# Grouping attention's PV matmuls by four column tiles, with new rules for ordering work and for sharing it with VectorE

## The chip, the cores and the metric

The kernel runs on one core of one Trainium2 chip. The metric is device time in microseconds (us), measured per execution; each figure is a median over several executions. On one core, a run is called slow when it is over 1.5% above the fastest run of the same kernel in its rounds. A profile is the record of one execution, and its span is a few us shorter than the measured time (965.3 against 967.4 us before). The profiled execution of the kernel before took 967.4 us, more than the median given below. "Granted clock" is TensorE's clock as the profile records it, as a share of full speed: the records hold only 1.00 and 0.50.

## The reference

One multi-query attention (32 query heads of width 16, one shared key and value head) over 2048 tokens of width 512, multiplied by a gate from a SwiGLU feed-forward network on the same normalised input:

```python
def _A_ref(x, wq, wk, wv, wo):            # S=2048, D=512, H=32, Dh=16
    q = (x @ wq).reshape(B, S, H, Dh).transpose(0, 2, 1, 3)
    k, v = x @ wk, x @ wv
    scores = jnp.einsum("bhqd,bkd->bhqk", q, k) * (Dh ** -0.5)
    p = softmax(scores, axis=-1)
    o = jnp.einsum("bhqk,bkd->bhqd", p, v)
    return o.transpose(0, 2, 1, 3).reshape(B, S, H * Dh) @ wo

def _B_ref(x, w_gate, w_up, w_down):      # F=1792
    return (silu(x @ w_gate) * (x @ w_up)) @ w_down

xn = layernorm(x)
return x + _A_ref(xn, ...) * silu(_B_ref(xn, ...))
```

All inputs are bfloat16.

## The kernel before

The attention runs in 32 blocks (16 groups of eight heads by 512 queries, each in two halves of four heads) of 16 steps, one step per 128 keys. A step makes two score tiles of 128x1024: four small matmuls, each with a contraction of 32 rows, so that they sit in four row groups of TensorE's array. The score tiles go into three ring buffers in PSUM. Most tiles are turned into probabilities by ScalarE (an exponential, written as bfloat16 into one of eight buffers `Pb`). Some go to VectorE, which builds the exponential from bit operations and two products: two score reads (`passA`), two masks (`dM`, `dE`) and two products (`dQ`, `dC`) for a pair of tiles, and three terms that the PV matmuls add up. The PV matmuls are 128x32: each uses 32 columns of the array, and four of them, one for each head, can sit in four column tiles (in the trace four that start together take 0.33 us, of the score matmuls as of PV, see below).

The order of instructions on each engine is fixed when the kernel is built, by a small list scheduler in the kernel's own Python. It knows a duration for each operation, and picks by priority (lower first): score matmuls and VectorE's score reads 0, exponentials, PV and the evictions of the feed-forward's PSUM bank 1, the "fill" matmuls of the feed-forward and projections 2.

```python
class _Sched:
    LAT = 0.13          # between two operations that depend on each other
    SWITCH = 0.09       # TensorE changes its kind of matmul
    ...
    def _pick(self, e):
        ...
        tm = max(t, min(o.ready for o in lst))
        best = min((o for o in lst if o.ready <= tm + 1e-9), key=lambda o: (o.prio, o.seq))
        if e in ("PE", "DVE"):
            soon = [o for o in lst if o.ready <= tm + 0.12 and o.prio[0] < best.prio[0]]
            if soon:
                best = min(soon, key=lambda o: (o.prio, o.seq))
        return max(t, best.ready), best
```

The loop over score tiles (k is the tile, two for each step) decides which tile VectorE gets, and issues PV as soon as one exponential is done, two matmuls at a time:

```python
        bl = sd.backlog["DVE"] + max(0.0, sd.free["DVE"] - now)
        if k >= 40 and st["last_d"] < k - 1:
            if st["d_half"] is None:
                if t <= BLK_T_D and bl < 2.5:
                    isD = True
            elif x != st["d_half"][0]:
                if bl < 2.5 or t >= NT - 3:
                    isD = True
        ...
        if not isD:
            ...
            ex = OP("ACT", 0.905, [scop, pdep, prev_exp], ..., name="exp")
            mms = [(VA[:, t, DH * half:DH * half + GRP], Pb[i][:, u * 512:(u + 1) * 512], 2 * x + u) for u in range(2)]
            pv = OP("PE", 0.23, [ex, o_rel[0], vdep], pv_emit(b, mms), (1, k), f"c{x}", "pv")
        else:
            ...   # passA; with the second tile of a pair also dM, dE, dQ, dC and twelve PV matmuls
```

The fill matmuls all go through one PSUM bank, `m_ps`: after four or more of them an eviction by ScalarE (tanh) and VectorE has to run before the next can start.

## Time and profile before

Before the change the median was 960.36 us over three runs (956.92 to 967.58).

| | before |
|---|---|
| span of the trace | 965.3 us |
| busy: TensorE, ScalarE, VectorE | 88%, 88%, 66% |
| score tiles on ScalarE, on VectorE | 868, 156 |
| mean granted clock | 0.949 |
| changes of kind on TensorE (score, PV, fill), from the instruction order; the trace gives the same | 2028 |

The first lines are the page's busy times and shares, and its 40 slices of the span. A digit is a tenth of a slice; `PEclk` is the granted clock in tenths.

```profile
PE 852.6 (88%) x5568; PEld 247.6 (26%) x5665; DVE 636.7 (66%) x771; ACT 850.3 (88%) x946; POOL 52.9 (5%) x64
...
ACT  2678798999999999999989999999999999799770
...
PEclk9858899999999999999999999999999999798795
```

Busy shares say that two engines are equally loaded, and not what their work costs. For this one reads starts. The timeline of the kernel before, around 405 us (columns: start, length, engine, line, operation, output and inputs, shape, count):

```profile
402.65 1.06 ACT L777 ACTIVATE Pb_126<-ring_97 128x1024 bf16<-128x1024 f32 x1
...
403.55 1.07 ACT L777 ACTIVATE Pb_127<-ring_98 128x1024 bf16<-128x1024 f32 x1
...
404.99 0.39 PE L763 MATMUL ring_98<-QB_119,KT_85 32*128 32x512 bf16 x2
...
405.31 0.39 PE L666 MATMUL o_ps<-Pb_127,VA 128*32 128x512 bf16 x2
...
405.63 0.39 PE L763 MATMUL ring_97<-QB_119,KT_85 32*128 32x512 bf16 x2
405.64 0.39 PE L763 MATMUL ring_96<-QB_119,KT_85 32*128 32x512 bf16 x2
...
405.96 0.39 PE L666 MATMUL o_ps<-Pb_128,VA 128*32 128x512 bf16 x2
```

An exponential is shown as 1.06 us long, but the next starts 0.90 us after it: the cost of one is 0.903 us, the smallest distance of two starts in the trace. On TensorE two score matmuls (404.99) hold the engine for 0.32 us until two PV matmuls start (405.31), which hold it for 0.32 us too. At 405.63 four score matmuls go together, in four row groups, and cost 0.33 us: as much as two. What runs side by side is nearly free here (0.33 us for four, 0.32 for two). Call a run of matmuls of one kind a **visit**, and its cost the smallest distance from its start to the start of the next kind; longer distances hold a wait, or matmuls that follow one another instead of starting together (in some visits of four PV matmuls of this trace the second two start 0.23 us after the first two, and the visit takes 0.54 us). A visit of two PV matmuls costs 0.325 us, one of four in four column tiles 0.331 us, one of twelve 0.764 us. Twelve are three sets of four, so a set takes about 0.21 us, which leaves about 0.11 us for each change of kind (both are estimates from 0.331 and 0.764 us).

With 0.903 us for an exponential and 0.477 for a tanh, ScalarE's work is 868 x 0.903 + 72 x 0.477 = 818 us. The first exponential starts at 20.5 us and the last at 934.7, so 914.2 us hold about 817 us of work. The other 97 us are **gaps**: the sum, over all pairs of ScalarE instructions between the first and the last exponential, of the distance of their starts less 0.903 us (or 0.477 us after a tanh).

The chain that ended last, by engine and by line, is the third view. PV matmuls (`o_ps L666`) are its largest item:

```profile
PE 52%; DVE 23%; ACT 9%; issue 7%; DMA 4%; SPq 3%; POOL 0%; DVEq 0%; ACTq 0%; POOLq 0%
PE o_ps L666 19%; PE m_ps L555 7%; PE ring_97 L763 6%; PE ring_98 L763 6%; PE ring_96 L763 6%; DVE Ub_129 L796 4%; PE m_ps L575 4%; DVE Ub_130 L796 3%; SPq L714 3%; DVE Wb_134 L814 2%; PE m_ps L442 1%; ACT th_135 L560 1%; DVE Wb_134 L817 1%; DVE Wb_133 L814 1%; ACT Pb_121 L777 1%
```

Last, stretches of time: busy us and number of instructions of each engine, then the granted clock.

```profile
core 0: us, PE busy (x) PEld busy (x) DVE busy (x) ACT busy (x) POOL busy (x), PEclk, DMA share, GB/s
0.00:118.00 118.00, 91.10 (x554) 27.72 (x562) 64.11 (x122) 78.29 (x88) 14.06 (x36) 0.83 0.23 78
...
300.00:500.00 200.00, 184.48 (x1227) 53.77 (x1246) 132.53 (x151) 192.32 (x216) 11.14 (x8) 1.00 0.05 12
500.00:700.00 200.00, 186.73 (x1271) 54.74 (x1290) 145.64 (x164) 192.75 (x216) 9.71 (x7) 1.00 0.04 10
```

In the middle TensorE is busy 92 to 93% and its clock is full. (Some matmul records are missing from this trace: 5568 matmuls against 5665 weight loads, so counts of matmuls in it are a little low.)

### The profile page before, as it was taken

How to read it: one execution, taken by the hardware profiler on the slowest of the kernel's cores; microseconds unless marked ns; L12 is line 12 of the kernel's file. 1: busy time of each engine (PE TensorE's matmuls, PEld its weight loads, DVE VectorE, ACT ScalarE, POOL GpSimd, SP SyncE). 2: the span in 40 equal slices, each digit the busy share in tenths (PEclk: the TensorE clock that was granted, in tenths of full speed). 3: DMA queues.
4: the chain of work that ended last, by engine and by line, in shares of the span. 5: the costliest groups of instructions: out<-in, count | busy, mean ns of one | idle time of the engine just before them, and what ended most of it. 6: DMA issues, size and time to landing. Idle time of an engine off the chain costs nothing.

```text
span 965.3 us, 14557 instructions
## 1 busy us (share of the span) xinstructions
PE 852.6 (88%) x5568; PEld 247.6 (26%) x5665; DVE 636.7 (66%) x771; ACT 850.3 (88%) x946; POOL 52.9 (5%) x64
## 2 busy tenths in 40 slices
PE   3799898988999999999989899998989999898980
PEld 1322222222222222222222222222222222222220
DVE  6416887878763567666775688897553558787553
ACT  2678798999999999999989999999999999799770
POOL 3100000000000100000000010000000110000001
PEclk9858899999999999999999999999999999798795
DMA  9000000000000100000000100000000000000001
GB/s 333 28 1 1 18 2 18 1 7 12 2 19 6 29 6 18 3 1 18 1 18 7 30 6 7 13 2 18 1 18 6 18 18 2 18 1 18 1 1 42
DMA packets 20109, 18.62 MB, mean 19 GB/s; under 512 B 9024, under 2 KB 15936, under 8 KB 20032
## 3 DMA queue, kind: packets, MB, share of 16 engines
q1 hardware_dynamic: 18448, 17.05, 5.8%
q8 instruction: 46, 0.75, 0.3%
q10 hardware_dynamic: 1584, 0.56, 0.2%
q14 instruction: 31, 0.25, 0.1%
HBM read 12.88 MB, written 2.36 MB: 16 GB/s over the span
## 4 chain that ended last, share of the span: by engine, by line
PE 52%; DVE 23%; ACT 9%; issue 7%; DMA 4%; SPq 3%; POOL 0%; DVEq 0%; ACTq 0%; POOLq 0%
PE o_ps L666 19%; PE m_ps L555 7%; PE ring_97 L763 6%; PE ring_98 L763 6%; PE ring_96 L763 6%; DVE Ub_129 L796 4%; PE m_ps L575 4%; DVE Ub_130 L796 3%; SPq L714 3%; DVE Wb_134 L814 2%; PE m_ps L442 1%; ACT th_135 L560 1%; DVE Wb_134 L817 1%; DVE Wb_133 L814 1%; ACT Pb_121 L777 1%
## 5 line engine op out<-in xcount | busy, mean ns | idle before, releaser
L666 PEld LDWEIGHTS <-VA 128*32 128x32 bf16 x1736 | 76.6, 94 | 185.7 <-issue 185.0
L763 PEld LDWEIGHTS <-KT_84 32*128 32x128 bf16 x1024 | 46.0, 92 | 168.4 <-issue 162.7
L763 PEld LDWEIGHTS <-KT_85 32*128 32x128 bf16 x1024 | 44.9, 91 | 158.0 <-issue 156.6
L555 PE MATMUL m_ps<-xnT,wg_sb 128*128 128x512 bf16 x204 | 65.7, 397 | 6.7 <-issue 2.4
L555 PE MATMUL m_ps<-xnT,wu_sb 128*128 128x512 bf16 x186 | 60.2, 389 | 9.3 <-DVE ab_137 L562 3.2
L575 PE MATMUL m_ps<-wd_sb,hT 128*128 128x512 bf16 x193 | 62.0, 392 | 4.9 <-issue 4.8
L796 DVE TENSOR_SCALAR Ub_130<-ring_98 128x1024 uint16<-128x1024 f32 x35 | 42.8, 1222 | 27.2 <-PE ring_98 L763 21.1
L796 DVE TENSOR_SCALAR Ub_129<-ring_97 128x1024 uint16<-128x1024 f32 x29 | 35.4, 1222 | 25.1 <-PE ring_97 L763 23.1
L814 DVE TENSOR_TENSOR Wb_134<-Wb_134 128x2048 f16<-128x2048 f16 x39 | 51.5, 1321 | 0.0
L817 DVE TENSOR_TENSOR Wb_134<-Wb_134,Ub_130 128x2048 f16<-128x2048 f16 x39 | 50.1, 1285 | 1.1
L796 DVE TENSOR_SCALAR Ub_129<-ring_98 128x1024 uint16<-128x1024 f32 x30 | 36.6, 1221 | 21.0 <-PE ring_98 L763 18.8
L777 ACT ACTIVATE Pb_121<-ring_98 128x1024 bf16<-128x1024 f32 x38 | 40.1, 1056 | 10.5 <-PE ring_96 L763 5.8
L777 ACT ACTIVATE Pb_125<-ring_97 128x1024 bf16<-128x1024 f32 x40 | 42.4, 1060 | 6.8 <-PE ring_97 L763 6.5
L814 DVE TENSOR_TENSOR Wb_133<-Wb_133 128x2048 f16<-128x2048 f16 x39 | 48.4, 1241 | 0.0
L817 DVE TENSOR_TENSOR Wb_133<-Wb_133,Ub_129 128x2048 f16<-128x2048 f16 x39 | 47.3, 1213 | 0.8
L777 ACT ACTIVATE Pb_121<-ring_96 128x1024 bf16<-128x1024 f32 x37 | 39.0, 1054 | 9.7 <-PE ring_97 L763 9.3
L777 ACT ACTIVATE Pb_122<-ring_96 128x1024 bf16<-128x1024 f32 x43 | 45.3, 1053 | 1.8 <-PE ring_98 L763 1.0
L666 PE MATMUL o_ps<-Pb_123,VA 128*32 128x512 bf16 x218 | 44.8, 408 | 0.6 <-DVE oa_138 L711 0.2
L777 ACT ACTIVATE Pb_127<-ring_96 128x1024 bf16<-128x1024 f32 x41 | 43.9, 1071 | 1.6 <-PE ring_96 L763 1.1
L666 PE MATMUL o_ps<-Pb_121,VA 128*32 128x512 bf16 x218 | 44.9, 408 | 0.3 <-DVE oa_138 L711 0.2
L666 PE MATMUL o_ps<-Pb_125,VA 128*32 128x512 bf16 x216 | 44.4, 408 | 0.7 <-DVE oa_139 L711 0.5
L666 PE MATMUL o_ps<-Pb_122,VA 128*32 128x512 bf16 x218 | 45.0, 410 | 0.0
(161 smaller groups left out, 2004.6 us busy)
## 6 DMA issues: line engine op xcount, KB each, us to landing
rb_142<-dscr_147 SPq DMA_DIRECT2D x8, 256.0 KB
rb_142<-dscr_148 SPq DMA_DIRECT2D x8, 256.0 KB
wg_sb<-in_B_w_gate_dram SPq DMA_DIRECT2D x1, 1792.0 KB
wu_sb<-in_B_w_up_dram SPq DMA_DIRECT2D x1, 1792.0 KB
wd_sb<-in_B_w_down_dram SPq DMA_DIRECT2D x1, 1792.0 KB, 19.8
x_sb<-in_A_x_dram SPq DMA_DIRECT2D x3, 512.0 KB
oa_138<-oa_139 SPq DMA_DIRECT2D x32, 32.0 KB, 2.0
oa_140<-oa_141 SPq DMA_DIRECT2D x32, 32.0 KB, 2.0
```

Source lines behind the costliest of these rows:

```text
L442: return [nc.tensor.matmul(out=dst, lhsT=wq_sb[:, kc, jj * P:(jj + 1) * P], rhs=xnT[:, kc, qs * 512:(qs + 1) * 512], start=(kc == 0), stop ...
L555: return lambda: [nc.tensor.matmul(out=m_ps[:], lhsT=w[:, kc, f * P:(f + 1) * P], rhs=xnT[:, kc, sc * 512:(sc + 1) * 512], start=(kc == 0) ...
L560: t_ = OP("ACT", 0.48, [a], lambda: nc.scalar.activation(out=th[i][:], in_=m_ps[:], func=ACT.Tanh, scale=0.5), (0,), name="tanh")
L575: return lambda: [nc.tensor.matmul(out=m_ps[:, :D], lhsT=hT[:, f, tt * P:(tt + 1) * P], rhs=wd_sb[:, f, :], start=(f == 0), stop=(f == FC ...
L666: r.append(nc.tensor.matmul(out=o_ps[GRP * g:GRP * g + GRP, :], lhsT=lhs, rhs=rhs, start=(n == 0), stop=(n == pv_total[(b, g)] - 1), tile_ ...
L714: return [nc.sync.dma_start(out=dn[DH * (2 * g + half):DH * (2 * g + half) + DH, pair, :], in_=oat[GRP * g + r0:GRP * g + r0 + 1, :]) for ...
L763: r.append(nc.tensor.matmul(out=tile_ps[:, u * 512:(u + 1) * 512], lhsT=KT[half][GRP * g:GRP * g + GRP, t * P:(t + 1) * P], rhs=QB[pair % ...
L777: ex = OP("ACT", 0.905, [scop, pdep, prev_exp], lambda i=i, tile_ps=tile_ps: nc.scalar.activation(out=Pb[i][:], in_=tile_ps[:], func=ACT.E ...
L796: pa = OP("DVE", 1.16, [scop, udep], lambda ui=ui, x=x, tile_ps=tile_ps: nc.vector.tensor_scalar(out=Ub[ui][:, x * 1024:(x + 1) * 1024], i ...
L814: e3 = OP("DVE", 1.16, [e1], lambda ei=ei: nc.vector.tensor_tensor(out=Wb[ei][:].bitcast(FP16), in0=Wb[ei][:].bitcast(FP16), in1=Wb[ei][:] ...
L817: e4 = OP("DVE", 1.16, [e3], lambda ui=ui, ei=ei: nc.vector.tensor_tensor(out=Wb[ei][:].bitcast(FP16), in0=Wb[ei][:].bitcast(FP16), in1=Ub ...
```

## The change

The intent has three parts. (1) **Joining**: PV matmuls are issued only in fours. In a step that ScalarE does alone, its two tiles are joined. In a step that it shares with VectorE it has only one tile, and that one is kept until the next shared step brings the other half. (2) **Picking rules**: TensorE and VectorE look ahead for a coming score operation (priority 0) and start other work only if this delays it by at most 2.0 us or 0.2 us; a dependence inside VectorE or GpSimd counts 0.08 us (before 0.13 us). On TensorE the limit of 2.0 us never binds, because the longest single operation in its plan counts about 1 us: in effect TensorE no longer idles up to 0.12 us for a coming score matmul. (3) **Share**: VectorE gets a tile whenever its queue of planned work is below 4.0 us (before 2.5, and not two tiles in a row).

```diff
 class _Sched:
+    SAME = {"DVE": 0.08, "POOL": 0.08}
+    GUARD = {"PE": 2.0, "DVE": 0.2}
...
-            lat = 0.0 if d.eng == op.eng == "PE" else self.LAT
+            lat = self.LAT if d.eng != op.eng else self.SAME.get(op.eng, 0.0)
...
-        if e in ("PE", "DVE"):
-            soon = [o for o in lst if o.ready <= tm + 0.12 and o.prio[0] < best.prio[0]]
-            if soon:
-                best = min(soon, key=lambda o: (o.prio, o.seq))
+        if e in self.GUARD:
+            hot = [o for o in lst if o.prio[0] <= 0 and o.ready > tm]
+            if hot and best.prio[0] > 0:
+                h = min(hot, key=lambda o: (o.ready, o.seq))
+                lim = h.ready + self.GUARD[e]
+                fit = [o for o in lst if o.ready <= tm + 1e-9 and tm + o.dur + self._sw(o) <= lim]
+                best = min(fit, key=lambda o: (o.prio, o.seq)) if fit else h
...
+    D_START, D_BL = 20, 4.0
...
-        if k >= 40 and st["last_d"] < k - 1:
-            if st["d_half"] is None:
-                if t <= BLK_T_D and bl < 2.5:
-                    isD = True
-            elif x != st["d_half"][0]:
-                if bl < 2.5 or t >= NT - 3:
-                    isD = True
+        if s >= D_START:
+            if st["d_half"] is None:
+                if t <= NT - 4 and bl < D_BL:
+                    dx = 0
+            elif bl < D_BL or t >= NT - 2:
+                dx = 1 - st["d_half"][0]
...
-            pv = OP("PE", 0.23, [ex, o_rel[0], vdep], pv_emit(b, mms), (1, k), f"c{x}", "pv")
+        todo = None
+        if dx is None:
+            todo = exps
+        elif half_pv is None:
+            half_pv = exps
+        else:
+            todo = dict(half_pv)
+            todo.update(exps)
+            half_pv = None
+        if todo is not None:
+            ...
+            pv = OP("PE", 0.25, [todo[x][0] for x in todo] + [o_rel[0], v_ready[c]], pv_emit(b, mms), (1, s), "c", "pv")
```

The rest of the diff rewrites the loop from tiles to steps and is left out.

More of the change, by code (lines that the diff above doesn't have):

```diff
@@ L209, in _arm, with _sw @@
         self.ready[op.eng].append(op)
+    def _sw(self, o):
+        return self.SWITCH if o.eng == "PE" and self.mode is not None and o.mode[0] != self.mode else 0.0
     def _pick(self, e):
@@ L646 @@
     st = {"d_half": None, "last_d": -9, "nA": 0, "nU": 0, "u": None, "nd": 0, "d0": None, "ev": None}
-    def slot_for(k):
-        best, bt = None, None
-        for i in range(3):
-            o = ring_rel[i]
-            t = o.end if o.start is not None else 1e6 + ring_age[i]
-            if best is None or t < bt:
-                best, bt = i, t
-        return best
     def pv_emit(b, mms):
@@ L670, in pv_emit @@
         return f
-    NB = NSC * NQ * 2
-    BLK_T_D = NT - 4
-    pend = {"norm": []}
+    D_START, D_BL = 20, 4.0
     ffn_list = []
@@ L728, in finish_block, with mm_of @@
             o_ready[pair // NQ] = m_
-    k = 0
     prev_exp = None
-    while k < NTILE:
-        b = k // TPB
-        t = (k % TPB) // 2
-        x = k % 2
+    half_pv = None
+    def mm_of(buf, w, i, t, half, gs):
+        r = []
+        for g in gs:
+            lhs = VA[:, t, DH * half:DH * half + GRP] if i is None else VD[:, i, t, DH * half:DH * half + GRP]
+            r.append((lhs, buf(g), g))
+        return r
+    for s in range(NTILE // 2):
+        b, t = s // NT, s % NT
         pair, half = b // 2, b % 2
-        if k % TPB == 0:
-            blk = {"pvs": [], "gcount": [0, 0, 0, 0]}
+        if t == 0:
+            pvs = []
+            half_pv = None
@@ L739 @@
             st["d_half"] = None
-        while gi < len(gates) and gates[gi][0] <= k:
+        while gi < len(gates) and gates[gi][0] <= 2 * s:
             gates[gi][2]()
             gi += 1
-        remaining = TPB - (k % TPB)
-        isD = False
         now = sd.free["PE"]
         bl = sd.backlog["DVE"] + max(0.0, sd.free["DVE"] - now)
-        if k >= 40 and st["last_d"] < k - 1:
+        dx = None
+        if s >= D_START:
             if st["d_half"] is None:
-                if t <= BLK_T_D and bl < 2.5:
-                    isD = True
-            elif x != st["d_half"][0]:
-                if bl < 2.5 or t >= NT - 3:
-                    isD = True
@@ L754 @@
-        c = t // 4
-        sl = slot_for(k)
-        tile_ps = ring[sl]
-        deps = [ring_rel[sl], k_ready[c][half], q_ready[pair]]
-        def sc_emit(tile_ps=tile_ps, x=x, t=t, half=half, pair=pair):
-            r = []
-            for u in range(2):
-                g = 2 * x + u
-                r.append(nc.tensor.matmul(out=tile_ps[:, u * 512:(u + 1) * 512],
-                                          lhsT=KT[half][GRP * g:GRP * g + GRP, t * P:(t + 1) * P],
-                                          rhs=QB[pair % 2][GRP * g:GRP * g + GRP, :],
-                                          start=True, stop=True, tile_position=(GRP * g, 0)))
-            return r
@@ L768 @@
-        scop = OP("PE", 0.23, deps + [last_sc], sc_emit, (0, k), f"r{x}", "sc")
-        last_sc = scop
-        kb_ready[b] = scop
-        vdep = v_ready[c]
-        lastt = k % TPB >= TPB - 2
-        if not isD:
+                if t <= NT - 4 and bl < D_BL:
+                    dx = 0
+            elif bl < D_BL or t >= NT - 2:
+                dx = 1 - st["d_half"][0]
+        c = t // 4
+        sls = []
+        for x in range(2):
+            best = None
+            for i in range(3):
+                if i in sls:
+                    continue
+                o = ring_rel[i]
+                key = o.end if o.start is not None else 1e6 + ring_age[i]
+                if best is None or key < best[0]:
+                    best = (key, i)
+            sls.append(best[1])
@@ new lines, with sc_emit @@
+        if dx == 0:
+            sls.reverse()
+        def sc_emit(sl, x, t=t, half=half, pair=pair):
+            return [nc.tensor.matmul(out=ring[sl][:, u * 512:(u + 1) * 512],
+                                     lhsT=KT[half][GRP * g:GRP * g + GRP, t * P:(t + 1) * P],
+                                     rhs=QB[pair % 2][GRP * g:GRP * g + GRP, :],
+                                     start=True, stop=True, tile_position=(GRP * g, 0))
+                    for u, g in enumerate((2 * x, 2 * x + 1))]
@@ L774 @@
+        scs = {}
+        for x in ((0, 1) if dx != 0 else (1, 0)):
+            scs[x] = OP("PE", 0.23, [ring_rel[sls[x]], k_ready[c][half], q_ready[pair], last_sc],
+                        lambda x=x, f=sc_emit, sl=sls[x]: f(sl, x), (0, s), f"r{x}", "sc")
+            last_sc = scs[x]
+        kb_ready[b] = last_sc
+        exps = {}
+        for x in range(2):
+            sl = sls[x]
+            ring_age[sl] = 2 * s + x
+            if x == dx:
+                continue
             i = st["nA"] % NPB
@@ L776 @@
             st["nA"] += 1
-            ex = OP("ACT", 0.905, [scop, pdep, prev_exp], lambda i=i, tile_ps=tile_ps: nc.scalar.activation(
-                out=Pb[i][:], in_=tile_ps[:], func=ACT.Exp, scale=escale, bias=ebias), (1, k), name="exp")
+            pb_rel.append(None)
+            ex = OP("ACT", 0.905, [scs[x], pdep, prev_exp], lambda i=i, sl=sl: nc.scalar.activation(
+                out=Pb[i][:], in_=ring[sl][:], func=ACT.Exp, scale=escale, bias=ebias), (1, s, x), name="exp")
             prev_exp = ex
             ring_rel[sl] = ex
-            mms = [(VA[:, t, DH * half:DH * half + GRP], Pb[i][:, u * 512:(u + 1) * 512], 2 * x + u) for u in range(2)]
-            pv = OP("PE", 0.23, [ex, o_rel[0], vdep], pv_emit(b, mms), (1, k), f"c{x}", "pv")
-            pb_rel.append(pv)
-            blk["pvs"].append(pv)
-        else:
-            st["last_d"] = k
+            exps[x] = (ex, i, st["nA"] - 1, t)
+        todo = None
[3 more added lines that the diff above has]
+            half_pv = exps
+        else:
+            todo = dict(half_pv)
+            todo.update(exps)
+            half_pv = None
+        if todo is not None:
+            mms = []
+            for x in sorted(todo):
+                ex, i, _, tt = todo[x]
+                mms += mm_of(lambda g, i=i: Pb[i][:, (g % 2) * 512:(g % 2 + 1) * 512], None, None, tt, half,
+                             (2 * x, 2 * x + 1))
+            pv = OP("PE", 0.25, [todo[x][0] for x in todo] + [o_rel[0], v_ready[c]], pv_emit(b, mms), (1, s), "c", "pv")
+            for x in todo:
+                pb_rel[todo[x][2]] = pv
+            pvs.append(pv)
+        if dx is not None:
+            sl = sls[dx]
             if st["d_half"] is None:
@@ L790 @@
                 st["nU"] += 1
-                part = 0
-            else:
-                part = 1
             ui = st["u"] % NU
             udep = ub_rel[st["u"] - NU] if st["u"] >= NU else None
-            pa = OP("DVE", 1.16, [scop, udep], lambda ui=ui, x=x, tile_ps=tile_ps: nc.vector.tensor_scalar(
-                out=Ub[ui][:, x * 1024:(x + 1) * 1024], in0=tile_ps[:], scalar1=ubias, scalar2=UINF,
-                op0=ALU.add, op1=ALU.min), (0, k), name="passA")
+            pa = OP("DVE", 1.16, [scs[dx], udep], lambda ui=ui, x=dx, sl=sl: nc.vector.tensor_scalar(
+                out=Ub[ui][:, x * 1024:(x + 1) * 1024], in0=ring[sl][:], scalar1=ubias, scalar2=UINF,
+                op0=ALU.add, op1=ALU.min), (0, s), name="passA")
             ring_rel[sl] = pa
-            if part == 0:
-                st["d_half"] = (x, t, pa)
+            if st["d_half"] is None:
+                st["d_half"] = (dx, t, pa)
             else:
@@ L804 @@
                 st["d_half"] = None
-                tx = {x0: t0, x: t}
+                tx = {x0: t0, dx: t}
                 ei = st["u"] % NE
                 edep = eb_rel[st["u"] - NE] if st["u"] >= NE else None
-                e1 = OP("DVE", 0.63, [pa, pa0, edep], lambda ui=ui, ei=ei: nc.vector.tensor_scalar(
+                e1 = OP("DVE", 0.62, [pa, pa0, edep], lambda ui=ui, ei=ei: nc.vector.tensor_scalar(
                     out=Wb[ei][:], in0=Ub[ui][:], scalar1=0x3FF, scalar2=0x3800, op0=ALU.bitwise_and,
-                    op1=ALU.bitwise_or), (2, k), name="dM")
-                e2 = OP("DVE", 0.63, [pa, pa0, edep], lambda ui=ui, ei=ei: nc.vector.tensor_scalar(
+                    op1=ALU.bitwise_or), (2, s), name="dM")
+                e2 = OP("DVE", 0.62, [pa, pa0, edep], lambda ui=ui, ei=ei: nc.vector.tensor_scalar(
                     out=Eb[ei][:], in0=Ub[ui][:], scalar1=0x7C00, scalar2=None, op0=ALU.bitwise_and),
-                    (2, k), name="dE")
-                e3 = OP("DVE", 1.16, [e1], lambda ei=ei: nc.vector.tensor_tensor(
+                    (2, s), name="dE")
+                e3 = OP("DVE", 1.18, [e1], lambda ei=ei: nc.vector.tensor_tensor(
                     out=Wb[ei][:].bitcast(FP16), in0=Wb[ei][:].bitcast(FP16), in1=Wb[ei][:].bitcast(FP16),
-                    op=ALU.mult), (2, k), name="dQ")
-                e4 = OP("DVE", 1.16, [e3], lambda ui=ui, ei=ei: nc.vector.tensor_tensor(
+                    op=ALU.mult), (2, s), name="dQ")
+                e4 = OP("DVE", 1.18, [e3], lambda ui=ui, ei=ei: nc.vector.tensor_tensor(
                     out=Wb[ei][:].bitcast(FP16), in0=Wb[ei][:].bitcast(FP16), in1=Ub[ui][:].bitcast(FP16),
-                    op=ALU.mult), (2, k), name="dC")
+                    op=ALU.mult), (2, s), name="dC")
                 mms = [(VD[:, i, tx[g // 2], DH * half:DH * half + GRP],
@@ L823 @@
                        for i, buf in enumerate((Eb[ei], Ub[ui], Wb[ei])) for g in range(4)]
-                pv = OP("PE", 0.72, [e4, e2, o_rel[0], v_ready[max(t0, t) // 4]], pv_emit(b, mms), (1, k), "c2", "dpv")
+                pv = OP("PE", 0.72, [e4, e2, o_rel[0], v_ready[max(t0, t) // 4]], pv_emit(b, mms), (1, s), "c", "dpv")
                 ub_rel.append(pv)
                 eb_rel.append(pv)
-                blk["pvs"].append(pv)
-        ring_age[sl] = k + 10
-        if lastt and x == 1:
-            finish_block(b, blk["pvs"])
-        while scop.start is None:
-            assert sd.step() is not None, (k, "stuck")
-        k += 1
+                pvs.append(pv)
+        if t == NT - 1:
+            assert half_pv is None and st["d_half"] is None
+            finish_block(b, pvs)
+        while last_sc.start is None:
+            assert sd.step() is not None, (s, "stuck")
     while gi < len(gates):
```

## The prediction

> **What bounds it now.** The trace spans 965.3 us (median of runs 960.4). Page part 1: TensorE and ScalarE both busy 88%, VectorE 66%. Starts in the timeline give real costs. A ScalarE exponential shows 1.06 us but the next starts 0.903 us later; a tanh takes 0.477. ScalarE's work is 868 x 0.903 + 72 x 0.477 = 818 us. Its first exponential starts near 21 us, the last ends at 936: 914 us hold those 818, with 96 us of gaps. Groups and waits put its idle time nearly all on score matmuls (64 us), mostly in the first 150 us and at 800-900 us. A fixed tail of 29 us follows.
>
> TensorE is the partner: a visit of two score matmuls costs 0.318 us, of two PV matmuls 0.325, of four PV matmuls in four column tiles 0.331, of twelve 0.765, of two fill matmuls 0.525 (start to start of the next kind). That is about 0.21 us for what streams side by side, plus 0.11 per change of kind. [...]four PV matmuls cost what two cost. The old instruction order has 2028 changes of kind and 638 PV visits of only two. TensorE needs roughly 790 us at full clock, more with the half-clock stretches (mean clock 0.949). Two engines, both 90% loaded, share three ring buffers and wait for each other.
>
> **What the change does** (instruction order of the new kernel):
> - PV visits fall from 807 to 481; visits of two from 638 to 1. Changes of kind fall from 2028 to 1527: 501 x 0.11 = 55 us. Streaming units fall by about 66 for scores and 312 for PV: 378 x 0.21 = 80 us. TensorE's need falls 135 us, to about 655.
> - 26 more score tiles go to VectorE (182 against 156): exponentials 868 to 842, so ScalarE needs 795 us. VectorE gets 13 more sets of about 6 us (two score reads at 1.2, two masks at 0.6, two products at 1.25): +78, to about 715 busy. The 104 added PV matmuls are counted above.
> - Fill work, prologue, tail, DMA: unchanged.
>
> **On the critical path.** TensorE's relief isn't worth 135 us: ScalarE becomes the only limit. Its 24 us come off directly. Of its 96 us of gaps I expect 50-60% to go, because scores no longer queue behind two-matmul PV visits; the rest stays (prologue, block ends, VectorE at over 80% holding ring buffers). Main phase 795 + 45 = 840, plus 21 + 29, gives 890 in a trace; median 892 us, range 866 to 924. Faster by over 2% 0.94, within 2% 0.04, slower 0.02.
>
> **What would show it.** Exponentials x842; TensorE busy 75-82%, ScalarE 90-93%, VectorE 79-82%; nearly all PV visits of four or more, 0.33 us each; ScalarE's gaps over 200-800 us halved; in the chain of waits a much larger ScalarE share and less PV. Tail still 29 us.
>
> **What would make it wrong.** (1) VectorE runs late (its scheduling durations are a few per cent below the measured 1.25 us products): score reads wait behind products, ring buffers stay held, exponentials starve; then 920-945. (2) The emptier TensorE gets a lower clock in the middle; a mean below 0.93 would show it. (3) Gaps in the first 150 us, set by the prologue on VectorE, don't shrink: +10 us. (4) Joined halves hold probability buffers longer.

## The result, and the profile after

The changed kernel is faster: 924.67 us median (917.6 to 926.24, four runs) against 959.12 us (956.92 to 967.58, four runs). The ratio is 0.961, with a 95% interval of 0.9545 to 0.9676. A ratio here is the mean time of one kernel's fast runs over the mean of the other's in the same rounds, so it is not quite the ratio of the medians. The forecast of 892 us was too low: 34 us of gain came instead of 68, and the median lies at the upper end of the stated range (866 to 924 us).

The page of the changed kernel, the same lines:

```profile
PE 787.4 (85%) x5769; PEld 231.2 (25%) x5769; DVE 709.9 (77%) x849; ACT 822.8 (89%) x920; POOL 58.1 (6%) x64
...
ACT  2688899999899999999999999999999999899850
...
PEclk9856799899799999999999999989999999799775
```

TensorE's busy time fell by 65 us and VectorE's rose by 73 us. The digit row of the clock now has an 8 or 7 in the middle, where before there were only nines. The stretches make this plainer:

```profile
0.00:118.00 118.00, 90.67 (x579) 27.07 (x580) 64.89 (x123) 81.43 (x92) 13.70 (x36) 0.78 0.23 78
118.00:300.00 182.00, 162.10 (x1202) 46.61 (x1201) 147.64 (x165) 173.19 (x195) 7.29 (x4) 0.93 0.03 9
300.00:500.00 200.00, 178.63 (x1353) 53.44 (x1353) 162.26 (x186) 194.30 (x220) 12.06 (x8) 0.97 0.05 12
500.00:700.00 200.00, 177.37 (x1360) 53.96 (x1358) 173.04 (x190) 193.35 (x218) 12.18 (x7) 0.97 0.04 12
```

From 300 to 700 us the granted clock was 1.00 before and is 0.97 now. That is the mean of a clock that is full most of the time and half for a few stretches, here of 3.4 or 6.8 us. In the whole of ScalarE's main phase the half-clock time rose from 75 to 133 us. The chain that ended last has less PV and more exponentials in it, as forecast:

```profile
PE 43%; ACT 25%; DVE 19%; issue 8%; DMA 3%; SPq 2%; POOL 0%; ACTq 0%; DVEq 0%; POOLq 0%
PE o_ps L665 11%; PE m_ps L563 7%; PE ring_98 L772 6%; PE ring_97 L772 6%; PE ring_96 L772 5%; DVE Ub_129 L824 4%; PE m_ps L583 4%; DVE Ub_130 L824 4%; ACT Pb_125 L793 3%; ACT Pb_126 L793 3%; ACT Pb_122 L793 3%; ACT Pb_128 L793 3%; ACT Pb_121 L793 3%; ACT Pb_124 L793 3%; ACT Pb_123 L793 3%
```

The timeline around one of the stretches at half clock, which the clock's records put at 603.7 to 610.5 us:

```profile
602.37 0.39 PE L665 MATMUL o_ps<-Pb_126,VA 128*32 128x512 bf16 x2
602.38 0.39 PE L665 MATMUL o_ps<-Pb_125,VA 128*32 128x512 bf16 x2
...
602.74 0.59 PE L563 MATMUL m_ps<-xnT,wu_sb 128*128 128x512 bf16 x2
...
603.26 0.39 PE L772 MATMUL ring_98<-QB_119,KT_85 32*128 32x512 bf16 x2
...
604.57 1.03 PE L563 MATMUL m_ps<-xnT,wu_sb 128*128 128x512 bf16 x2
...
605.54 0.61 PE L772 MATMUL ring_96<-QB_119,KT_85 32*128 32x512 bf16 x2
...
606.28 1.22 ACT L793 ACTIVATE Pb_125<-ring_96 128x1024 bf16<-128x1024 f32 x1
606.63 0.61 PE L772 MATMUL ring_98<-QB_119,KT_85 32*128 32x512 bf16 x2
...
607.17 1.89 PE L563 MATMUL m_ps<-xnT,wg_sb 128*128 128x512 bf16 x4
...
608.99 0.61 PE L772 MATMUL ring_97<-QB_119,KT_85 32*128 32x512 bf16 x2
609.09 0.60 ACT L568 ACTIVATE th_135<-m_ps 128x512 f32<-128x512 f32 x1 [1.59 <-PE m_ps L563]
```

Two PV visits' worth of matmuls start within 0.01 us of each other at 602.37: joining works. A pair of fill matmuls starts at 602.74 and the score matmuls behind it at 603.26, 0.52 us later. At half clock the same pair holds TensorE from 604.57 to the next score at 605.54, 0.97 us. At 607.17 four fill matmuls in a row hold it for 1.82 us, the next score tile comes at 608.99, and ScalarE, which started its last exponential at 606.28, finds nothing to do for 1.59 us, until the fill matmuls release a tanh.

Where the time of the two kernels lies (all in us; "half" means that the clock was half when the later of the two ScalarE instructions started or 1 us earlier):

| | before | changed |
|---|---|---|
| up to the first exponential | 20.5 | 20.8 |
| ScalarE's work in the main phase | 817 | 794 |
| gaps, first 118 us | 25.9 | 22.1 |
| gaps after that, at full clock | 57.6 | 24.9 |
| gaps after that, at half clock | 13.5 | 30.0 |
| after the start of the last exponential | 30.5 | 31.4 |

Call a stretch in which the clock falls to half a **drop**. After the first 118 us the changed kernel has 15 gaps of over 1 us, all 15 of them in or just after half clock. At full clock ScalarE loses 3.7% of the time, at half clock 31.7%. The stretch from 200 to 800 us shows the exchange most cleanly. Before, it had 42.1 us of gaps and not one drop of the clock. Now it has 20.7 us of gaps in 538 us at full clock (3.8% of the time, before 7.0%), and 21.2 us in 62 us at half clock, around nine drops. So as much came back at half clock as had gone at full clock. Since the profiled execution of the kernel before was 8 us over its median, some of the 42.1 us may not be typical of it.

### The profile page after: what moved, and what is told of

It reads as the page before. It is cut to its first block, busy times and chain, and to the rows that moved or that the text cites. A ratio compares the mean times of both kernels' runs of the same rounds, so it can differ in the third digit from the quotient of the medians.

```text
span 922.9 us, 14837 instructions
## 1 busy us (share of the span) xinstructions
PE 787.4 (85%) x5769; PEld 231.2 (25%) x5769; DVE 709.9 (77%) x849; ACT 822.8 (89%) x920; POOL 58.1 (6%) x64
## 4 chain that ended last, share of the span: by engine, by line
PE 43%; ACT 25%; DVE 19%; issue 8%; DMA 3%; SPq 2%; POOL 0%; ACTq 0%; DVEq 0%; POOLq 0%
PE o_ps L665 11%; PE m_ps L563 7%; PE ring_98 L772 6%; PE ring_97 L772 6%; PE ring_96 L772 5%; DVE Ub_129 L824 4%; PE m_ps L583 4%; DVE Ub_130 L824 4%; ACT Pb_125 L793 3%; ACT Pb_126 L793 3%; ACT Pb_122 L793 3%; ACT Pb_128 L793 3%; ACT Pb_121 L793 3%; ACT Pb_124 L793 3%; ACT Pb_123 L793 3%
## 5 line engine op out<-in xcount | busy, mean ns | idle before, releaser
L772 PEld LDWEIGHTS <-KT_84 32*128 32x128 bf16 x1024 | 51.0, 92 | 193.9 <-issue 186.9
L772 PEld LDWEIGHTS <-KT_85 32*128 32x128 bf16 x1024 | 50.3, 92 | 181.5 <-issue 179.1
L563 PE MATMUL m_ps<-xnT,wu_sb 128*128 128x512 bf16 x224 | 69.5, 404 | 4.0 <-DVE ab_137 L570 2.4
L583 PE MATMUL m_ps<-wd_sb,hT 128*128 128x512 bf16 x224 | 67.7, 391 | 5.5 <-DVE g_sb L591 5.4
L824 DVE TENSOR_SCALAR Ub_129<-ring_98 128x1024 uint16<-128x1024 f32 x37 | 45.2, 1223 | 31.9 <-PE ring_98 L772 28.3
L665 PEld LDWEIGHTS <-VA 128*32 128x32 bf16 x1684 | 42.9, 94 | 106.5 <-issue 106.2
L824 DVE TENSOR_SCALAR Ub_129<-ring_97 128x1024 uint16<-128x1024 f32 x38 | 46.5, 1223 | 24.9 <-PE ring_97 L772 16.3
L842 DVE TENSOR_TENSOR Wb_134<-Wb_134 128x2048 f16<-128x2048 f16 x45 | 58.7, 1305 | 0.0
L845 DVE TENSOR_TENSOR Wb_133<-Wb_133,Ub_129 128x2048 f16<-128x2048 f16 x46 | 57.9, 1259 | 0.8
L842 DVE TENSOR_TENSOR Wb_133<-Wb_133 128x2048 f16<-128x2048 f16 x46 | 57.1, 1240 | 0.0
L845 DVE TENSOR_TENSOR Wb_134<-Wb_134,Ub_130 128x2048 f16<-128x2048 f16 x45 | 55.8, 1240 | 0.7
L793 ACT ACTIVATE Pb_121<-ring_96 128x1024 bf16<-128x1024 f32 x39 | 42.7, 1095 | 10.4 <-PE ring_97 L772 8.6
L824 DVE TENSOR_SCALAR Ub_130<-ring_97 128x1024 uint16<-128x1024 f32 x33 | 40.3, 1222 | 13.4 <-PE ring_97 L772 6.1
L824 DVE TENSOR_SCALAR Ub_130<-ring_98 128x1024 uint16<-128x1024 f32 x30 | 36.7, 1222 | 17.5 <-PE ring_98 L772 13.3
L793 ACT ACTIVATE Pb_121<-ring_98 128x1024 bf16<-128x1024 f32 x35 | 38.3, 1094 | 9.4 <-PE ring_96 L772 7.7
L568 ACT ACTIVATE th_135<-m_ps 128x512 f32<-128x512 f32 x56 | 37.3, 667 | 9.3 <-PE m_ps L563 9.3
L824 DVE TENSOR_SCALAR Ub_130<-ring_96 128x1024 uint16<-128x1024 f32 x27 | 33.0, 1221 | 15.8 <-PE ring_96 L772 9.1
L793 ACT ACTIVATE Pb_128<-ring_97 128x1024 bf16<-128x1024 f32 x40 | 43.9, 1098 | 0.9 <-PE ring_97 L772 0.8
L665 PE MATMUL o_ps<-Pb_121,VA 128*32 128x512 bf16 x212 | 44.4, 416 | 0.3 <-ACT Pb_121 L793 0.3
L665 PE MATMUL o_ps<-Pb_128,VA 128*32 128x512 bf16 x210 | 44.4, 419 | 0.3 <-DVE oa_139 L708 0.2
L665 PE MATMUL o_ps<-Pb_127,VA 128*32 128x512 bf16 x210 | 44.4, 419 | 0.0
```

Of the source, the lines that this page charges most:

```text
L563: return lambda: [nc.tensor.matmul(out=m_ps[:], lhsT=w[:, kc, f * P:(f + 1) * P], rhs=xnT[:, kc, sc * 512:(sc + 1) * 512], start=(kc == 0) ...
L568: t_ = OP("ACT", 0.48, [a], lambda: nc.scalar.activation(out=th[i][:], in_=m_ps[:], func=ACT.Tanh, scale=0.5), (0,), name="tanh")
L583: return lambda: [nc.tensor.matmul(out=m_ps[:, :D], lhsT=hT[:, f, tt * P:(tt + 1) * P], rhs=wd_sb[:, f, :], start=(f == 0), stop=(f == FC ...
L665: r.append(nc.tensor.matmul(out=o_ps[GRP * g:GRP * g + GRP, :], lhsT=lhs, rhs=rhs, start=(n == 0), stop=(n == pv_total[(b, g)] - 1), tile_ ...
L772: return [nc.tensor.matmul(out=ring[sl][:, u * 512:(u + 1) * 512], lhsT=KT[half][GRP * g:GRP * g + GRP, t * P:(t + 1) * P], rhs=QB[pair % ...
L793: ex = OP("ACT", 0.905, [scs[x], pdep, prev_exp], lambda i=i, sl=sl: nc.scalar.activation(out=Pb[i][:], in_=ring[sl][:], func=ACT.Exp, sca ...
```

## The experiments

**Theory (clock).** Joining empties TensorE (busy for 787 us, before 853), and its clock suffers from that (133 us of half clock, before 75). At half clock TensorE is again the limit (busy 99% of that time from 200 to 800 us, at full clock 88%) and ScalarE starves. **Rival (order).** The gaps come from the planned order, a late VectorE and score work stuck behind other work; half clock comes with such places and is only their sign.

Of the clock the traces before and after show this: only full and half appear in its records, and the stretches at half clock, but for the last, which the end of the record cuts, are multiples of 3.41 us (6.8, 3.4, 10.2 and 13.7 us after the first 118 us of the changed kernel). What sets the clock they do not show; that it falls with what TensorE does is the theory, which the next runs test.

### Full-array dummies, and the same dummies on a sixteenth of the array

The first pair of runs puts 159 dummy matmuls ahead of score matmuls. A dummy writes the ring bank that the score matmul then overwrites, so the results stay the same. The dummies go where the scheduler's plan shows low activity (matmul time weighted by the part of the array used) in the 3.41 us before. The limit in the edit, 0.42, and the weights are settings; no run shows them to be figures of the clock. The choice of VectorE's tiles is written down, so that the rest of the order is exactly that of the changed kernel.

The edit, shortened, with its constants written in:

```diff
+            if o.name == "sc":
+                n = 0
+                while n < 2 and sum(a[1] for a in act) < 0.42 * 3.41:
+                    act.append((o.start, 0.213))
+                    chain("PE", dummy(o.slot))
+                    n += 1
# e1_warm
+        return nc.tensor.matmul(out=ring[sl][:, 0:512], lhsT=xnT[:, 0, 0:P], rhs=xnT[:, 0, 0:512], start=True, stop=True)
# e2_placebo: a 32x32 corner of the array in its place
+        return nc.tensor.matmul(out=ring[sl][0:GRP, 0:512], lhsT=xnT[0:GRP, 0, 0:GRP], rhs=xnT[0:GRP, 0, 0:512],
+                                start=True, stop=True, tile_position=(0, 0))
```

> The changed kernel with its share of VectorE written down step by step (same order) and 159 dummy 128x128 matmuls, 512 columns each, put ahead of score matmuls where the array's planned activity over the last 3.4 us is below 0.42; each writes the ring bank that the score then overwrites, so the result is the same. Clock theory (the remaining gaps come from half-clock stretches[...]): half-clock time falls from 133 us to under 60, mean clock above 0.945, ScalarE's gaps from 77 us to about 50-60, time 900-912 us although TensorE gets about 40-50 us more work. Rival (the gaps come from the planned order and VectorE's lateness, and half clock is only a sign of them): time 924 or longer, gaps as before or more.

> As the run before, but each of the 159 dummies uses only a 32x32 tile of the array, so that it takes the same place and time on TensorE and adds a sixteenth of the activity. Clock theory: no gain, half-clock time stays at 120-140 us, time 925-940 us. Rival (the dummies help by spacing of the order, not by activity): same time as with full dummies.

Full dummies: 920.49 us (four runs, 909.04 to 924.74; before in the same rounds 962.0). Small dummies: 961.06 us (958.98 to 973.4). Both correct. Each median is over four runs of which one is called slow; the three fast ones lie at 909.04 to 922.37 us and at 958.98 to 962.01 us. (Against the kernel before, the record's verdict on these two is "unclear", at ratios of 0.954 and 1.000; the comparison here is of the two with each other, and there all runs of the one are below all runs of the other.) The two programs have the same instructions at the same places, and at full clock both kinds of dummy cost nearly the same: the smallest distance from a dummy to the score matmul behind it is 0.308 us in one and 0.303 us in the other. Only behind a fill matmul is a small dummy dearer, as it is a change of kind there and a full one is not (0.306 us against 0.215 us from the fill matmul to the dummy); with some 20 such places in the traces that is about 2 us. They differ by 40.6 us in time, and by 109 us in half-clock time (48 against 157 us in the main phase). The stretches of the run with full dummies:

```profile
118.00:300.00 182.00, 162.30 (x1205) 47.75 (x1223) 146.00 (x166) 172.56 (x194) 7.95 (x5) 0.95 0.04 10
...
500.00:700.00 200.00, 177.61 (x1378) 55.04 (x1397) 172.08 (x190) 195.36 (x219) 13.47 (x8) 1.00 0.04 12
```

and of the run with small ones:

```profile
118.00:300.00 182.00, 163.93 (x1121) 43.84 (x1140) 136.62 (x154) 161.27 (x179) 5.75 (x4) 0.86 0.03 8
...
500.00:700.00 200.00, 180.24 (x1309) 53.06 (x1328) 164.95 (x183) 186.06 (x208) 12.43 (x8) 0.94 0.04 10
```

With a clock of 0.95 and 1.00, ScalarE executed 194 and 219 instructions; with 0.86 and 0.94, 179 and 208. Order and slots being equal, the rival can't explain this. The clock costs time by itself, and dummies on the whole array keep it up where dummies on a sixteenth of it don't (48 against 157 us of half clock). The sizes in the expectation were off: full dummies came out 4 us below the changed kernel, which is within the scatter of either (909.04 to 924.74 and 917.6 to 926.24 us) and not the 12 to 24 us expected, and small ones lost 36 us, not 1 to 16. A dummy on the way to a score tile is dear: gaps at full clock rose from 24.9 to 37.0 us.

### The parts of the change, undone one at a time

> The changed kernel with the same share of VectorE, tile by tile, and the same picking rules, but PV matmuls of ScalarE's halves issued two at a time as each exponential ends, not joined to four. If joining is the main part of the gain: time 945-970 us, as slow as the kernel before or slower. If the gain comes from the share and the picking rules: time below 935 us.

> The changed kernel with the same share of VectorE and joined PV, but the old rule for picking the next operation (look ahead 0.12 us, no guard for score work, no same-engine latency). If the picking rules carry a large part: 945 us or more. If they are a detail: 920-932 us.

The first takes back joining, the second the picking rules; in both VectorE's tiles are those of the changed kernel, written down.

```diff
# e3_pairs: for each exponential
+            pv = OP("PE", 0.23, [ex, o_rel[0], v_ready[c]], pv_emit(b, mms), (1, s), f"c{x}", "pv")
# e4_oldpick
-        if e in self.GUARD:
-            ...
+        if e in ("PE", "DVE"):
+            soon = [o for o in lst if o.ready <= tm + 0.12 and o.prio[0] < best.prio[0]]
+            ...
```

Without joining: 1024.1 us (1018.99 to 1046.82), ratio to before 1.064. Without the picking rules: 978.4 us (971.54 to 983.32), ratio 1.019. Both are far slower than the changed kernel, so with this share neither joining nor the picking rules can be left out. The second falls into its first expectation (945 us or more); the first is 54 us above the longest time that its expectation named. Forcing the larger share on a kernel without joining is harsh, since that share had been planned for a freer TensorE.

> The changed kernel with one number changed: VectorE takes a tile only when less than 2.4 us of work is queued for it, not 4.0, so that it gets 152 of 1024 score tiles (before 156, changed kernel 182) and ScalarE 872; joining and picking rules kept. If the larger share is worth what it takes off ScalarE: 30 exponentials x 0.903 = 27 us longer, so about 945-955 us. If the share matters little because TensorE or the clock sets the pace: within 10 us of 924.

```diff
-    D_START, D_BL = 20, 4.0
+    D_START, D_BL = 20, 2.4
```

The smaller share with joining and the picking rules: 986.33 us over four runs from 968.39 to 1012.96. Three of these are called slow, as they are over 1.5% above the fastest, and the profiled run is one of them, so no ratio is given, and the 62 us over the changed kernel are not to be taken as the worth of the share. All four are longer than the changed kernel's median by over 40 us, where 27 were expected from ScalarE's added work: neither expectation held. The profile has 290 us of half clock. The fastest of the four runs had the highest mean clock (0.872) and the slowest the lowest (0.803).

> The changed kernel with PV issued two matmuls at a time as in the second of the decompositions before, but the share of VectorE left to the rule (queue under 4 us), which now gives it 116 tiles instead of 182, not forced to the written list. If joining is worth most of the gain even when the share may adapt: 945-975 us. If the forced list was what made that earlier run so slow and the picking rules alone are a gain: 920-940 us. Clock theory: TensorE is fuller, so half-clock time under 90 us.

> Joining alone: PV in fours, but the old picking rules and a queue limit of 2 us, which gives VectorE 154 tiles (before: 156). If joining alone brings the gain: 920-940 us. If an emptier TensorE with the old order just falls to half clock more often: 960-1000 us, half-clock time over 200 us.

```diff
# e9_pairs_own: the edit of e3_pairs, with the rule for the share left as it is
# e10_join_only: the edit of e4_oldpick, and
-    D_START, D_BL = 20, 4.0
+    D_START, D_BL = 20, 2.0
```

New rules without joining: 961.48 us (954.91 to 967.17), ratio to before 1.003, the same. Joining without the new rules, at about the share of the kernel before (154 tiles): 1018.09 us (1016.17 to 1023.85), ratio 1.062, slower. The first lies in its first expectation, and its half-clock time is 41 us (under 90 expected); the second is beyond the 960 to 1000 us of its second expectation, with 311 us of half clock (over 200 expected). The stretches of the kernel without joining:

```profile
300.00:500.00 200.00, 184.36 (x1174) 55.23 (x1192) 104.85 (x122) 195.78 (x221) 9.64 (x8) 1.00 0.05 12
500.00:700.00 200.00, 183.44 (x1154) 54.42 (x1174) 96.19 (x113) 198.72 (x225) 8.84 (x7) 1.00 0.04 10
```

and of the one with joining alone:

```profile
300.00:500.00 200.00, 172.57 (x1153) 47.42 (x1174) 126.96 (x144) 177.67 (x198) 8.56 (x6) 0.85 0.03 9
500.00:700.00 200.00, 172.80 (x1110) 46.10 (x1120) 122.17 (x141) 174.20 (x193) 9.41 (x8) 0.81 0.04 12
```

These two show more of what each part does. With the new rules and unjoined PV the clock stays at 1.00 after the first 118 us, and from 200 to 800 us ScalarE has 23.3 us of gaps, against 42.1 before. So the gaps are nearly halved without joining; whether by the picking rules or by the smaller share of VectorE was not tried apart. TensorE is busy 92% of the time from 300 to 700 us, and the rule for the share can give VectorE only 116 tiles, so ScalarE has 908 exponentials: 40 more than before, or 36 us, against the 46 us that its gaps lost. (That balance is of the traces, and this kernel's profile is of its fastest run, 954.91 us, while that of the kernel before is of a long one. In the medians the two amounts cancel.) Joining is what makes room on TensorE for 182 tiles on VectorE: from this run to the changed kernel, which differ in joining alone, ScalarE's work falls by 59 us and its gaps rise by 26 us: 30 us more at half clock, where there were none after the first 118 us, and a little less at full clock.

With joining alone ScalarE has 21.3 us of gaps at full clock from 200 to 800 us. That is no halving, since only 377 of these 600 us count as full clock: it is 5.6% of them, against 7.0% before and 3.9% with the new rules and unjoined PV. For 205 us the clock is half, with another 73.6 us of gaps. An emptier TensorE was worth less than nothing there.

### Keeping the clock up without added work

If the clock is the rest, it should help to spread the work that uses the whole array. In the changed kernel fill matmuls come in bursts, then wait for the eviction of `m_ps` (at 538.38 us four come together, after 0.65 us in which TensorE idled until VectorE's eviction had ended). The next experiment hands out pairs of fill matmuls at least 1.7 us apart in the plan, and puts the evictions of `m_ps` first in VectorE's queue. It adds no instruction of another kind; the rule for the share then gives VectorE 184 tiles.

```diff
# shortened, with the constant written in
         for emit, dur, deps in parts:
+            pace[0] = max(pace[0] + 1.7, sd.free["PE"])
+            deps = deps + [ext(pace[0])]
...
-            out=ab[i][:], in0=th[i][:], ..., op1=ALU.mult), (1,), name="silu")
+            out=ab[i][:], in0=th[i][:], ..., op1=ALU.mult), (0,), name="silu")
# and the same for the other four evictions of m_ps
```

> The changed kernel with fill matmuls handed out at least 1.7 us apart per pair and their evictions put first in VectorE's queue[...]; no instruction added. Clock theory: fewer drops to half clock in the middle (13 now), half-clock time 90-110 us, time 908-920 us. Rival (planned order and a late VectorE): score reads on VectorE now wait behind evictions, so no gain, 922-935 us.

> As the run before, plus 89 full-array dummies ahead of score matmuls where planned activity over 3.4 us is still below 0.38. Clock theory: half-clock time under 50 us with about half of the dummies of the first experiment, time 898-912 us, the fastest of all. Rival: dummies cost what they give, 915-930 us.

> The changed kernel with full-array dummies only in the first 125 us and after 810 us of the planned order (60 of them), none in the middle. Clock theory: half clock in the first 118 us falls from 51 to under 10 us, ScalarE's gaps there from 22 to about 14 us, time 910-918 us; the drops in the middle stay.

Paced fill: 910.69 us (904.65 to 911.07), ratio to before 0.944; half-clock time 102 us instead of 133, both as its clock theory expected, and from 200 to 800 us six drops instead of nine and 13.0 us of gaps at half clock instead of 21.2. Gaps at full clock there are unchanged (21.3 against 20.7). All four runs are below all eight runs of the changed kernel (917.6 to 926.24 us, the repeat below included). The two edits of this run were not tried apart.

Paced fill with 89 dummies (the edit of the first run with the limit set to 0.38): 914.85 us (912.57 to 926.28), half-clock time 61 us. The clock is higher and the time isn't lower, so the expectation failed: the dummies cost what they gave.

The changed kernel with 60 dummies at both ends only (`o.start < 125 or o.start > 810`): 925.63 us (919.45 to 927.02), no gain where 910 to 918 us were expected. In the first 118 us the gaps fell from 22.1 to 14.0 us as expected, but the later gaps at half clock rose from 30.0 to 37.8 us. (Two profiles of the unedited changed kernel differ by 4.5 us in this measure, see the table.)

> The paced-fill kernel (910.7 us) plus 43 full-array dummies in the first 125 us only, where the earlier run with dummies at both ends had ScalarE's gaps fall from 22 to 14 us. Clock theory: half-clock time in the first 118 us from 62 to under 10 us, ScalarE's gaps there from 22 to about 14 us, time 900-907 us. Against it: what is won there is lost later and the time stays at 908-915 us.

> The changed kernel itself, unedited, on the same chip as these runs: 918-928 us, half-clock time 110-140 us. It shows how far the measured differences exceed what one kernel shows from chip to chip.

```diff
# e11_evsp_early: paced fill, and the dummies of e1_warm only early in the plan
+            if o.name == "sc" and o.start < 125:
```

Paced fill with 43 dummies early: 901.49 us (898.21 to 908.36), ratio to before 0.940 (0.9313 to 0.9485), correct. The changed kernel on the same chip, unedited: 922.66 us (921.8 to 924.4), half-clock time 120 us, as expected. The early dummies, lost on the changed kernel, seem to be kept on the paced one: gaps in the first 118 us are 14.9 us instead of 22.3, and the later ones do not rise. By the times alone the step from the paced kernel is not shown: the two were run in different rounds, single runs overlap (904.65 to 911.07 and 898.21 to 908.36 us), and so do the intervals of their ratios (0.937 to 0.951 and 0.931 to 0.949). It has the lowest median. Its early stretch and its middle:

```profile
0.00:118.00 118.00, 90.02 (x663) 30.64 (x674) 69.40 (x129) 88.12 (x100) 14.09 (x36) 0.96 0.23 78
...
500.00:700.00 200.00, 175.82 (x1362) 53.74 (x1385) 171.74 (x194) 196.94 (x223) 10.90 (x7) 0.99 0.04 12
```

All kernels together. "Work" is ScalarE's (the number of exponentials times 0.903, plus 34 us for the tanhs); "later" is after the first 118 us. Times are medians over all runs, slow ones included; the other columns come from each one's one profile.

| kernel | us | exponentials | work | gaps, first 118 us | later, full clock | later, half clock | half-clock time |
|---|---|---|---|---|---|---|---|
| before | 959.12 | 868 | 818 | 25.9 | 57.6 | 13.5 | 75 |
| changed | 924.67 | 842 | 795 | 22.1 | 24.9 | 30.0 | 133 |
| e1 full dummies | 920.49 | 842 | 795 | 13.9 | 37.0 | 20.6 | 48 |
| e2 small dummies | 961.06 | 842 | 795 | 28.7 | 29.6 | 56.5 | 157 |
| e3 not joined, share forced | 1024.1 | 842 | 795 | 24.0 | 64.4 | 85.4 | 171 |
| e4 old picking, share forced | 978.4 | 842 | 795 | 24.6 | 43.7 | 61.7 | 239 |
| e5 smaller share (slow runs) | 986.33 | 872 | 822 | 29.0 | 19.2 | 61.3 | 290 |
| e6 paced fill | 910.69 | 840 | 793 | 22.3 | 24.1 | 18.1 | 102 |
| e7 paced fill, dummies | 914.85 | 840 | 793 | 13.9 | 30.9 | 24.2 | 61 |
| e8 dummies at the ends | 925.63 | 842 | 795 | 14.0 | 26.4 | 37.8 | 102 |
| e9 not joined, share adapts | 961.48 | 908 | 854 | 22.5 | 28.3 | 0.0 | 41 |
| e10 joined only | 1018.09 | 870 | 820 | 17.9 | 34.3 | 92.2 | 311 |
| e11 paced fill, early dummies | 901.49 | 840 | 793 | 14.9 | 24.6 | 14.8 | 48 |
| e12 changed, again | 922.66 | 842 | 795 | 23.5 | 26.1 | 25.5 | 120 |

**What stays open.** What the clock follows isn't settled. That the part of the array used counts is shown by the two runs with dummies (48 against 157 us of half clock). How much work keeps the clock full is not shown: in the changed kernel it fell to half twelve times between 118 and 870 us, and in the 3.41 us before each fall 10 to 24 matmuls started and TensorE was never idle for over 1.57 us at a time. Nor is it shown what matmuls that run side by side do for the clock, and so whether joining by itself lowers it: of the kernels with unjoined PV and the new rules, e9 has 41 us of half clock and e3, with more tiles on VectorE, has 171. Open too is why the gain of the early dummies was lost in e8 and kept in e11, and how much of e6's gain is pacing and how much the order of evictions.

## Why the prediction was right or wrong

- **Right: faster, and how.** The direction held. Exponentials are 842 as read from the order, ScalarE's work fell by the 24 us forecast, VectorE's busy time is 710 us (715 forecast), and all but one of the 481 PV visits hold at least four matmuls, at 0.331 us for four where nothing has to be waited for. Four PV matmuls cost what two cost: 0.331 against 0.325 us.
- **Mis-sized: "Of its 96 us of gaps I expect 50-60% to go".** That is the term that failed. It put 45 us of gaps into the main phase; the trace has 77. These 32 us are nearly the whole difference between 890 us and the trace's 922.9; the start and the tail add 2 us. At full clock the forecast held even so: from 200 to 800 us, gaps at full clock went from 42.1 to 20.7 us, from 7.0% of that time to 3.8%. What was left out is the 21.2 us that came back in the same stretch at half clock.
- **Wrong in the same step: no price for the clock in the sum.** Danger (2), "The emptier TensorE gets a lower clock in the middle; a mean below 0.93 would show it", was named, and it came: 0.914 in the profiled run, 0.912 to 0.937 in all. The main sum counted it at nothing. That the clock costs time by itself is shown by the two runs with dummies: same places, nearly the same cost at full clock, 109 us of half clock and 40.6 us between them.
- **Wrong: what joining is worth.** The text put the halved gaps down to scores no longer queueing behind visits of two PV matmuls. The run without joining and with the new rules (e9) has gaps as short (23.3 us from 200 to 800 us), so that the halving at full clock came as forecast but not for the reason given: that is luck. Joining pays through the share: 182 tiles on VectorE with it, 116 without, under the same rule. The forecast took the 182 tiles from the plan and counted their 24 us, but not as joining's doing.
- **Wrong in the busy shares.** TensorE at 85% was forecast at 75 to 82%. Half clock, where TensorE is busy 99% of the time from 200 to 800 us, is not the main reason: at full clock in the same stretch it is busy 88%, against 93% before. Its busy time fell by 65 us, where its need was forecast to fall by 135; why is open. ScalarE at 89% and VectorE at 77% are just below their ranges, as the span is longer than forecast.
- **Danger (1), a late VectorE, did not come.** Products that depend on each other start 1.25 us apart in the trace; the scheduler counts 1.18 + 0.08 = 1.26. The worry compared the wrong numbers. The waits of score matmuls for VectorE's score reads sum to 15.0 us, before to 9.7 us. **Danger (3)** came in part: gaps in the first 118 us shrank only from 25.9 to 22.1 us. **Danger (4)** did not come: of the waits before ScalarE's instructions 46.8 us end with score matmuls and 9.3 us with fill matmuls, and none with PV.

## What to carry to other kernels

Price instructions by the distance of their starts, visit by visit: here four PV matmuls in four column tiles cost 0.331 us where two cost 0.325, and a change of kind about 0.11 us (the estimate above). When a change takes work off TensorE, count its clock in the sum: here the granted clock went from 0.949 to 0.914, and after the first 118 us half clock took back half of the gaps that the change had closed (32.7 us fewer at full clock, 16.5 more at half). Spreading the remaining full-array work evenly, with its evictions put first, won more than adding dummy work to the changed kernel (910.69 against 920.49 us). And test parts of a change in company as well as alone: here joining alone, or the new rules without joining, gained nothing over the kernel before, and all three parts together gained 34 us.
